# Due dates and measured ways in a hand-written planner: the first two blocks of a convolution with ELU layers

## The chip, the cores and the metric

One core of one Trainium2 chip runs the whole kernel as one launch. The metric is device time in microseconds (us) of that launch: the median of several runs. Engines are named PE (TensorE), DVE (VectorE), ACT (ScalarE), POOL (GpSimd) and SP (SyncE, which here only issues transfers).

## The reference

The inputs are x of 4 x 4096 x 192 and generated weights of 4 x 4096 x 8 x 7. Each token takes the softmax of its seven weights per head, and sums the last seven tokens with them (a causal convolution whose weights differ by token). The result goes through two matrices with an ELU between them:

```python
w = np.exp(weight_gen - np.max(weight_gen, axis=-1, keepdims=True))
w = w / (np.sum(w, axis=-1, keepdims=True) + 1e-09)
x_pad = np.concatenate([np.zeros((B, K - 1, D)), x], axis=1)
x_unf = x_pad[:, np.arange(S)[:, None] + np.arange(K)[None, :], :].reshape(B, S, K, H, D // H)
y = np.einsum('bshk,bskhg->bshg', w, x_unf).reshape(B * S, D)
h = y @ w_in                      # 192 x 2048
g = np.where(h > 0.0, h, np.exp(np.minimum(h, 0.0)) - 1.0)
out = g @ w_out                   # 2048 x 192
```

## The kernel before

The 16384 tokens go through in 32 blocks of 512, and each block takes 8 steps, one for each pair of 128-wide slices of the 2048 hidden units: 256 steps. A step multiplies into two PSUM banks of a ring of four (`h`, line 661, or line 657 for the two halves of step 0), ACT and DVE make the ELU of them (lines 718 to 732), and two steps later PE multiplies the result with w_out (line 689) into accumulator banks.

Block 0 multiplies in plain fp32, with decoded weights (`m_in`, `m_out`). From block 1 on every operand is split into two fp32r parts, hi and lo.

The matrices arrive as 64-bit floats and are turned into fp32 on the core. A piece of w_in or w_out is loaded by SP (lines 349, 384), ACT reads its two words (309, 312), DVE does three operations on it (315, 318, 321), and POOL adds the last part (331 for w_in, 325 for w_out). This happens beside block 0, piece by piece.

The convolution of blocks 0 and 1 is summed on PE: DVE makes a product `v` (line 555) for each of the seven taps and each half of the tokens, and PE adds it up with the identity matrix (line 542), in one bank for each half (`acc`, `accd`). Of block 0's second half POOL does the last three taps (`pa`, `pb`, lines 484 and 526). From block 2 on the convolution is on POOL. The products of block 0 read the softmax weights from a PSUM bank, which line 467 fills; ACT copies them to `wg` (line 470) for POOL. The result is transposed by DVE (line 605) and, for block 0, copied across partition halves by ACT and DVE (line 622).

Before any data is there, PE runs 21 multiplications of the identity matrix with itself (`turn_over`, line 402).

What sets the order is `Plan`. Every instruction, or small group, is a task with an engine and an estimated cost. A task that has a due date hands it back to the tasks it needs, less its cost and the way from engine to engine (`HOP`, or `SAME` within one engine). The tasks are then placed in the order of their due dates, each in the first free gap of its engine, and emitted in the order of the starts that this gives. Every engine runs its own instructions in that order. `port` is a resource that POOL tasks and some DVE tasks hold one at a time. The planned times have no other effect: waits on the chip follow the data.

Step k is due at 15,500 ns plus `FIRST[k]` for the first eleven steps and then one `STEP` (4,396 ns) after the other. `FIRST` thus places the early work against each other, and all later work against the early work.

Of the kernel before, what the change touches and what calls it, by code (L numbers as in the profile page):

```python
# [22 lines left out]
class Ring:  # L23


    def __init__(self, pool, shape, dtype, name, bufs):
        self.make = lambda dtype=dtype: pool.tile(
            list(shape), dtype, tag=name, name=name, bufs=bufs)
        self.bufs, self.made = bufs, []
# [23 lines left out]
class Plan:  # L53
# [4 lines left out]

    HOP = {"hop": 200, "dma": 2200, "pe": 250, "act": 220, "dve": 220, "pool": 220}
    SAME = {"hop": 0, "dma": 0, "pe": 0, "act": 60, "dve": 60, "pool": 60}

    def __init__(self):
        self.tasks = []

    def add(self, engine, cost, run, reads=(), writes=(), due=None, port=False):
        t = Task(engine, cost, run, due, port or engine == "pool")
        for h in reads:
            t.needs.update(h.writers)  # L70
        for h in writes:
            t.needs.update(h.users)
            if not h.users:
                if h.make:
                    t.makes.append(h)
                if h.before:
                    t.needs.update(h.before.users)
        for h in (*reads, *writes):
            h.users.append(t)
        for h in writes:  # L80
            h.writers.append(t)
        t.needs.discard(t)
        t.at = len(self.tasks)
        self.tasks.append(t)
        return t

    def lag(self, a, b):

        return self.SAME[a.engine] if a.engine == b.engine else self.HOP[a.engine]

    def issue(self):
        for t in self.tasks:
            for n in t.needs:
                n.next.append(t)
        for t in reversed(self.tasks):
            due = [n.due - t.cost - self.lag(t, n) for n in t.next]
            if t.due is not None:
                due.append(t.due)
            t.due = min(due)
        taken = {e: [(-1, 0)] for e in (*self.HOP, "port")}  # L100

        def fit(busy, at, cost):

            i = bisect.bisect_right(busy, (at, float("inf"))) - 1
            at = max(at, busy[i][1])
            while i + 1 < len(busy) and busy[i + 1][0] < at + cost:
                i += 1
                at = max(at, busy[i][1])
            return at

        for t in sorted(self.tasks, key=lambda t: (t.due, t.at)):
            uses = [taken[e] for e in ((t.engine, "port") if t.port else (t.engine,))]
            at = max([n.start + n.cost + self.lag(n, t) for n in t.needs], default=0)
            while True:
                to = at
                for busy in uses:
                    to = fit(busy, to, t.cost)
                if to == at:
                    break
                at = to  # L120
            t.start = at
            for busy in uses:
                bisect.insort(busy, (at, at + t.cost))
        self.emit(sorted(self.tasks, key=lambda t: (t.start, t.due, t.at)))
# [9 lines left out]
def conv_elu_kernel(  # L134
# [11 lines left out]
    nc = tc.nc  # L146
# [29 lines left out]
    PLAIN = 8  # L176
    EARLY = {0: 2500, 1: 1000}
    SPARE = 4
    FIRST = (0, 2667, 5719, 10622, 15932, 27986, 36877, 42127, 47378, 52168, 57525)
    ON_VEC = range(5, NF // 2)  # L180

    def rows(ap, t0, n):

# [49 lines left out]
    r_acc = [ring(f"acc{i}", [P, N], 1, pool=ps) for i in range(2)]  # L233
    r_accd = [ring(f"accd{i}", [P, N], 1, pool=ps) for i in range(2)]

    plan = Plan()
    add = plan.add

    idle = r_acc[0].new()
# [168 lines left out]
    def chunk(blk):  # L408

        n, t0 = J, blk * J * S  # L410
        xw, wg, wm, ws = r_xw.new(), r_wg.new(), r_wm.new(), r_ws.new()
        wg_h[blk] = wg
        xw_h[blk] = xw
        k, kk = n * H, n * H * K

        def w():
            return wg.t[:, 0:n]

        def wide(h):
            return h.t.to_broadcast([P, n, H, K])  # L420

        def load(to, src, n, d, at=0, both=False, only=quadrants()):
            def run():
                for p, s, q in only:
                    eng = nc.scalar if both and q else nc.sync
                    eng.dma_start(out=to()[p], in_=rows(src, t0 + s * J + at, n)[  # L426
                        :, :, q * d:(q + 1) * d])
            return run

        def load_w(only=quadrants()):  # L430
            return load(lambda: w().rearrange("p t h k -> p t (h k)"), weight_gen, n, H * K,
                        both=blk == 0, only=only)

        if blk == 0:
            add("dma", max(dma(P * n, H * K * 4), Q * S * ISSUE // 2), load_w(), writes=[wg], due=-2)
        for one in quadrants() if blk else ():
            add("dma", max(dma(A * n, H * K * 4), ISSUE), load_w([one]), writes=[wg])
        if blk == 0:
            xw_h[blk] = xw = [xw, Handle()]
            m = n + HALO  # L440
            for i, (a, b) in enumerate(((0, m - JH), (m - JH, m))):
                add("dma", max(dma(P * (b - a), DQ * 4), Q * S * ISSUE),
                    load(lambda a=a, b=b: xw[0].t[:, a:b], x, b - a, DQ, a),
                    writes=[xw[i]], due=-1 + i)
        else:
            for one in quadrants():
                add("dma", max(dma(A * (n + HALO), DQ * 4), ISSUE),
                    load(lambda: xw.t, x, n + HALO, DQ, only=[one]), writes=[xw])
        add("dve", dve(kk), lambda: nc.vector.tensor_reduce(
            out=wm.t[:, :, :, 0], in_=w(), axis=AX.X, op=ALU.max), reads=[wg], writes=[wm])  # L450
        add("dve", dve(kk), lambda: nc.vector.tensor_tensor(
            out=w(), in0=w(), in1=wide(wm), op=ALU.subtract), reads=[wm], writes=[wg], port=True)
        add("act", act(kk), lambda: nc.scalar.activation(
            out=w(), in_=w(), func=ACTF.Exp), writes=[wg])
        add("dve", dve(kk), lambda: nc.vector.tensor_reduce(
            out=ws.t[:, :, :, 0], in_=w(), axis=AX.X, op=ALU.add), reads=[wg], writes=[ws])
        add("act", act(k), lambda: nc.scalar.activation(
            out=ws.t, in_=ws.t, func=ACTF.Copy, bias=1e-9), writes=[ws])
        add("dve", 6.4 * k + 60, lambda: nc.vector.reciprocal(out=ws.t, in_=ws.t),
            writes=[ws])  # L460
        if blk == 0:
            h = wb_h[blk] = r_h.new()

            def bank():
                return h.t[:, 0:kk].rearrange("p (t h k) -> p t h k", h=H, k=K)

            add("dve", dve(kk), lambda: nc.vector.tensor_tensor(
                out=bank(), in0=w(), in1=wide(ws), op=ALU.mult), reads=[ws, wg], writes=[h],
                port=True)
            add("act", act(kk, True), lambda: nc.scalar.copy(out=w(), in_=bank()),  # L470
                reads=[h], writes=[wg])
            return
        add("dve", dve(kk), lambda: nc.vector.tensor_tensor(  # L473
            out=w(), in0=w(), in1=wide(ws), op=ALU.mult), reads=[ws], writes=[wg], port=True)
# [30 lines left out]
    def summed(blk, s0, own):  # L505
# [6 lines left out]
        xws = xws if blk == 0 else [xws]  # L512
        xw = xws[0]
        cs = [r_acc[1].new(), r_accd[1].new()]
        wb = [wb_h[blk]] * 2 if blk == 0 else cs[::-1]
        w0 = JH * DQ
        WK = JH * H * K
        rests = []
# [10 lines left out]
            rests.append(rest)  # L529

        def bank_w(i):
            at = i * WK if blk == 0 else w0
            return wb[i].t[:, at:at + WK]

        for i in range(2) if blk else ():
# [323 lines left out]
    with tc.manual_schedule():  # L859

        nc.vector.memset(scratch, 0.0)
        add("act", 1500, lambda: nc.scalar.activation(out=scratch, in_=scratch, func=ACTF.Exp),
            due=2500)
        make_identity(nc, ident)
        turn_over(21)
        for s in range(len(todo) + LAG):
            now = todo[s] if s < len(todo) else None
            up = todo[s - LAG] if s >= LAG else None
            if now:
                blk, k = now  # L870
                if k == 0:
                    chunk(blk)
                    if blk < 2:
                        summed(blk, s, OWN[blk])
                    else:
                        conv(blk, s)
                if blk == 0:
                    if k in in_pieces:
                        weights_in(k, in_pieces[k])
                    weights_out(k)  # L880
            period(s, now, up)
            if up and up[1] == NP - 1:
                drain(up[0], s)
        plan.issue()
# [34 lines left out]
```

## Time and profile before

| | us |
|---|---|
| median of 3 runs (1166.26 to 1166.52) | 1166.32 |
| the profiled execution, its own time | 1165.96 |
| its span, first to last instruction | 1164.2 |

The profile is of one execution; its own time is 1.76 us more than the span. PE is busy for 99% of the span, DVE for 71%, ACT for 77% and POOL for 59%. A matmul's end is modelled, so a wait of PE shows best in the distance from one group's start to the next. The profiler counts an fp32 matmul as two records. Matmuls of the two partition halves (64*128) run side by side.

### The profile page before, as it was taken

What the parts mean: (1) busy time and instruction counts of PE and PEld (TensorE: products, weight loads), DVE (VectorE), ACT (ScalarE), POOL (GpSimd) and SP (SyncE); (2) the same over time, 40 slices, a digit from 0 to 9 for tenths busy, and PEclk for the clock granted to TensorE, in tenths of its full rate; (3) what the DMA queues carried; (4) which work ended last, traced back from release to release, by engine and by line L of the source; (5) the groups of instructions that cost most, each with busy time, mean ns of one, the idle gap of its engine ahead of it and who ended that gap; (6) DMA issues with size and microseconds to landing.
All of it is one profiled execution on the core that took longest, in us unless ns stands there. A gap on an engine that the chain in (4) does not pass through costs nothing.

```text
span 1164.2 us, 32346 instructions
## 1 busy us (share of the span) xinstructions
PE 1157.0 (99%) x12858; PEld 1053.8 (91%) x12858; DVE 828.8 (71%) x1501; ACT 894.8 (77%) x1794; POOL 690.1 (59%) x424
## 2 busy tenths in 40 slices
PE   9999999999999999999999999999999999999998
PEld 6689999999999999999998999999999999999997
DVE  7967767866776776776787677687677776667564
ACT  6768778878777778777877777887877877777775
POOL 4576596388559858658859858756567655500000
PEclk9999999999999999999999999999999999999999
DMA  7831233323323332213332223332222211111100
GB/s 185 171 71 42 56 70 70 70 48 68 80 46 67 70 70 47 62 33 70 70 70 60 60 50 69 71 69 57 63 50 47 65 43 30 28 29 42 42 16 15
DMA packets 143128, 71.05 MB, mean 61 GB/s; under 512 B 98816, under 2 KB 141824, under 8 KB 142976
## 3 DMA queue, kind: packets, MB, share of 16 engines
q1 hardware_dynamic: 142112, 68.72, 26.7%
q8 instruction: 101, 1.65, 0.6%
q14 instruction: 51, 0.42, 0.1%
q10 hardware_dynamic: 864, 0.25, 0.1%
HBM read 31.98 MB, written 12.58 MB: 38 GB/s over the span
## 4 chain that ended last, share of the span: by engine, by line
PE 96%; DVE 2%; SPq 1%; DMA 0%; issue 0%; ACT 0%; POOL 0%; DVEq 0%; POOLq 0%; ACTq 0%
PE h L661 46%; PE accd L689 25%; PE acc L689 25%; PE accd L542 0%; SPq L426 0%; SPq L349 0%; DVE v L555 0%; DMA raw_in<-in_moe_w_in 0%; DVE hi L723 0%; DVE m_in L321 0%; DMA xw<-in_x 0%; DVE lo L730 0%; ACT e L718 0%; POOL m_in L331 0%; DVE m_in L318 0%
## 5 line engine op out<-in xcount | busy, mean ns | idle before, releaser
L723 DVE SCALAR_TENSOR_TENSOR h<-e,h 128x512 f32<-128x512 f32 x496 | 319.8, 690 | 221.1 <-ACT e L720 221.0
L718 ACT ACTIVATE e<-h 128x512 f32<-128x512 f32 x512 | 278.6, 595 | 184.6 <-PE h L661 184.4
L661 PE MATMUL h<-xhi,WI 64*128 64x512 f32 x2976 | 417.4, 394 | 0.1
L730 DVE TENSOR_TENSOR lo<-h,hi 128x512 fp32r<-128x512 f32 x496 | 322.1, 685 | 87.4 <-ACT hi L728 81.9
L661 PEld LDWEIGHTS h<-xhi,WI 64*128 64x128 f32 x2976 | 302.9, 185 | 47.8 <-DVE lo L730 0.7
L689 PE MATMUL accd<-WO,hi 64*128 64x384 f32 x1984 | 330.9, 357 | 0.0
L689 PE MATMUL acc<-WO,hi 64*128 64x384 f32 x1984 | 329.6, 355 | 0.0
L728 ACT CAST hi<-h 128x512 fp32r<-128x512 f32 x496 | 278.1, 597 | 41.7 <-DVE h L723 34.1
L720 ACT ACTIVATE e<-e 128x512 f32<-128x512 f32 x512 | 299.0, 644 | 0.1
L689 PE MATMUL acc<-WO,lo 64*128 64x192 f32 x1984 | 293.6, 249 | 0.0
L689 PE MATMUL accd<-WO,lo 64*128 64x192 f32 x1984 | 292.8, 248 | 0.0
L500 POOL TENSOR_TENSOR pa<-pa,pb 128x768 f32<-128x768 f32 x150 | 282.0, 1880 | 13.5 <-DVE pb L484 2.0
L484 POOL TENSOR_TENSOR pb<-xw,wg 128x768 f32<-128x768 f32 (+1 forms) x179 | 277.1, 1548 | 12.1
L689 PEld LDWEIGHTS acc<-WO,hi 64*128 64x128 f32 x1984 | 242.3, 185 | 4.5
L689 PEld LDWEIGHTS acc<-WO,lo 64*128 64x128 f32 x1984 | 237.6, 187 | 2.4
L661 PE MATMUL h<-xlo,WI 64*128 64x512 f32 x1488 | 239.3, 390 | 0.0
L689 PEld LDWEIGHTS accd<-WO,lo 64*128 64x128 f32 x1984 | 237.6, 188 | 0.0
L689 PEld LDWEIGHTS accd<-WO,hi 64*128 64x128 f32 x1984 | 233.5, 184 | 0.0
L661 PEld LDWEIGHTS h<-xlo,WI 64*128 64x128 f32 x1488 | 164.4, 184 | 28.2
L484 POOL TENSOR_TENSOR pa<-xw,wg 128x768 f32<-128x768 f32 (+1 forms) x31 | 47.5, 1532 | 176.2 <-DVE wg L473 148.1
L500 POOL TENSOR_TENSOR xc<-pa,pb 128x768 f32<-128x768 f32 x30 | 55.5, 1851 | 106.0 <-DVE xt L605 104.4
L605 DVE STREAM_TRANSPOSE xt<-xc 128x256 f32<-128x256 f32 x90 | 33.0, 416 | 1.4
(84 smaller groups left out, 495.2 us busy)
## 6 DMA issues: line engine op xcount, KB each, us to landing
xw<-in_x SPq DMA_DIRECT2D x124, 168.0 KB, 3.5
xhi<-xhi SPq DMA_DIRECT2D x62, 192.0 KB, 3.1
xlo<-xlo SPq DMA_DIRECT2D x62, 192.0 KB, 2.9
out_dram<-raw_out SPq DMA_DIRECT2D x124, 96.0 KB, 1.9
wg<-in_weight_gen SPq DMA_DIRECT2D x126, 28.0 KB, 2.2
raw_out<-in_moe_w_out SPq DMA_DIRECT2D x8, 384.0 KB, 5.9
raw_in<-in_moe_w_in SPq DMA_DIRECT2D x12, 192.0 KB, 4.3
raw_in<-in_moe_w_in SPq DMA_DIRECT2D x8, 96.0 KB, 2.5
```

Of the source, the lines that this page charges most:

```text
L484: lambda: eng.tensor_tensor(out=h.t[:, 0:J], in0=xw.t[:, j0 + k:j0 + k + J, :].rearrange("p j (h g) -> p j h g", g=G), in1=wg.t[:, j0:j0 + ...
L500: add("pool", pool(J * DQ), lambda b=b, to=to: nc.gpsimd.tensor_tensor(out=to.t, in0=a.t, in1=b.t, op=ALU.add), reads=[b] if to is a else ...
L605: nc.vector.transpose(out=xt(i)[:, c], in_=src[:, :, c * A:(c + 1) * A])
L661: return lambda: nc.tensor.matmul(out=h.t, lhsT=w_in_f[k][1]()[p, c] if w is None else WI[p, k, w, c], rhs=x.t[p, c, c0:c0 + 2].rearrange( ...
L689: return nc.tensor.matmul(out=to(), lhsT=src.t[p, g * P:(g + 1) * P], rhs=w, start=start, stop=False, skip_group_check=True).ins
L718: add("act", act(N, True), lambda: nc.scalar.activation(out=e.t, in_=h.t, func=ACTF.Relu, scale=-1.0), reads=[h], writes=[e])
L720: add("act", act(N), lambda: nc.scalar.activation(out=e.t, in_=e.t, func=ACTF.Exp, scale=-1.0), writes=[e])
L723: add("dve", dve(N), lambda: nc.vector.scalar_tensor_tensor(out=to.t, in0=e.t, scalar=-1.0, in1=h.t, op0=ALU.add, op1=ALU.max), reads=[e, ...
L728: add("act", act(N, True), lambda: nc.scalar.copy(out=hi.t, in_=h.t), reads=[h], writes=[hi])
L730: add("dve", dve(N), lambda: nc.vector.tensor_tensor(out=lo.t, in0=h.t, in1=hi.t.bitcast(F32), op=ALU.subtract), reads=[h, hi], writes=[lo])
```

## The change

It alters the numbers that the planner works with, and one piece of the program.

- `HOP` and `SAME`, the ways from engine to engine, have new values, and one from DVE to POOL its own.
- The costs of the first three loads, of the softmax weights and of the two parts of block 0's x, are other numbers.
- `FIRST` has new values; from the seventh entry on they are later, the last by 7,475 ns.
- `NUDGE` moves the due dates of 168 tasks forward, by 200 to 4,000 ns each. Tasks are named by their number in the order in which the program adds them; the numbers go from 12 to 682, which is into block 3. The task's forerunners inherit the earlier date.
- The softmax weights of block 0 are written into two PSUM banks, one for each half of the tokens, by two DVE instructions of 112 columns where there was one of 224. ACT copies the second half alone, since POOL reads nothing else.
- `turn_over` runs 14 multiplications instead of 21.

```diff
-    HOP = {"hop": 200, "dma": 2200, "pe": 250, "act": 220, "dve": 220, "pool": 220}
-    SAME = {"hop": 0, "dma": 0, "pe": 0, "act": 60, "dve": 60, "pool": 60}
+    HOP = {"hop": 200, "dma": 2200, "pe": 220, "act": 140, "dve": 130, "pool": 100}
+    SAME = {"hop": 0, "dma": 0, "pe": 0, "act": 20, "dve": 125, "pool": 65}
...
+        if a.engine == "dve" and b.engine == "pool":
+            return 220
...
-            t.due = min(due)
+            t.due = min(due) - self.nudge.get(t.at, 0)
...
-    FIRST = (0, 2667, 5719, 10622, 15932, 27986, 36877, 42127, 47378, 52168, 57525)
+    FIRST = (0, 2700, 5400, 10600, 15900, 28000, 37500, 42900, 48300, 55000, 65000)
...
+    NUDGE = {
+        12: 3400, 22: 2700, 32: 1800, 41: 2200, 44: 3700, 46: 2700, 48: 2000, 50: 2600, 56: 1400,
+        58: 3800, 67: 2500, 71: 1600, 72: 3800, 79: 1700, 84: 1400, 96: 2600, 97: 3000, 98: 1200,
...
+        470: 1600, 471: 2200, 472: 2500, 474: 2400, 475: 600, 476: 3200, 479: 3200, 480: 3500,
+        481: 1800, 482: 2700, 485: 1600, 486: 1100, 487: 1800, 488: 2700, 490: 200, 498: 2300,
...
-            add("dma", max(dma(P * n, H * K * 4), Q * S * ISSUE // 2), load_w(), writes=[wg], due=-2)
+            add("dma", 700 + Q * S * ISSUE // 2, load_w(), writes=[wg], due=-2)
...
-                add("dma", max(dma(P * (b - a), DQ * 4), Q * S * ISSUE),
+                add("dma", dma(P * (b - a), DQ * 4),
...
-            h = wb_h[blk] = r_h.new()
-
-            def bank():
-                return h.t[:, 0:kk].rearrange("p (t h k) -> p t h k", h=H, k=K)
-
-            add("dve", dve(kk), lambda: nc.vector.tensor_tensor(
-                out=bank(), in0=w(), in1=wide(ws), op=ALU.mult), reads=[ws, wg], writes=[h],
-                port=True)
-            add("act", act(kk, True), lambda: nc.scalar.copy(out=w(), in_=bank()),
-                reads=[h], writes=[wg])
+            wb_h[blk] = [r_h.new(), r_h.new()]
+            for i, h in enumerate(wb_h[blk]):
+                def half(t, i=i):
+                    return t[:, i * JH:(i + 1) * JH]
+
+                def bank(h=h):
+                    return h.t[:, 0:kk // 2].rearrange("p (t h k) -> p t h k", h=H, k=K)
+
+                add("dve", dve(kk // 2), lambda half=half, bank=bank: nc.vector.tensor_tensor(
+                    out=bank(), in0=half(w()), in1=half(wide(ws)), op=ALU.mult),
+                    reads=[ws, wg], writes=[h], port=True, due=due1(0) - 14000 + 1000 * i)
+                if OWN[blk][i] < K:
+                    add("act", act(kk // 2, True), lambda half=half, bank=bank: nc.scalar.copy(
+                        out=half(w()), in_=bank()), reads=[h], writes=[wg])
...
-        wb = [wb_h[blk]] * 2 if blk == 0 else cs[::-1]
+        wb = wb_h[blk] if blk == 0 else cs[::-1]
...
-            at = i * WK if blk == 0 else w0
+            at = 0 if blk == 0 else w0
...
-        turn_over(21)
+        turn_over(14)
```

## Rows read from the trace of the kernel before

**Rows 1.** The page: the span.

```profile
span 1164.2 us, 32346 instructions
```

**Rows 2.** Stretches: us, then busy us (count) of each engine, clock, DMA.

```profile
8.05:16.25 8.20, 7.96 (x27) 4.29 (x25) 8.08 (x19) 3.74 (x7) 5.58 (x6) 1.00 0.86 212
16.25:24.93 8.68, 8.59 (x49) 5.02 (x49) 8.26 (x15) 7.60 (x15) 4.26 (x5) 1.00 0.91 235
24.93:37.05 12.12, 12.11 (x105) 8.77 (x104) 11.64 (x24) 11.27 (x25) 6.56 (x7) 1.00 0.90 179
37.05:45.39 8.34, 7.57 (x25) 4.01 (x23) 8.27 (x19) 7.77 (x17) 5.38 (x7) 1.00 0.72 149
75.00:1100.00 1025.00, 1024.89 (x11672) 946.85 (x11670) 731.73 (x1318) 801.82 (x1609) 649.72 (x384) 1.00 0.26 58
```

**Rows 3.** Timeline of PE to 60 us: start, length, operation, count, wait.

```profile
8.05 4.73 PE L542 MATMUL acc<-v,ident 128*128 128x384 f32 x14
...
16.25 2.86 PE L657 MATMUL h<-xhi,m_in 64*128 64x256 f32 x24 [0.24 <-POOL m_in L331]
19.19 5.76 PE L661 MATMUL h<-xhi,m_in 64*128 64x512 f32 x24
...
26.33 2.74 PE L661 MATMUL h<-xhi,m_in 64*128 64x512 f32 x12
...
31.68 2.85 PE L661 MATMUL h<-xhi,m_in 64*128 64x512 f32 x12
...
37.05 4.78 PE L542 MATMUL acc<-v,ident 128*128 128x384 f32 x14
42.61 2.85 PE L542 MATMUL accd<-v,ident 128*128 128x384 f32 x8 [0.77 <-DVE v L555]
45.39 2.85 PE L661 MATMUL h<-xhi,m_in 64*128 64x512 f32 x12
...
53.00 2.74 PE L661 MATMUL h<-xhi,m_in 64*128 64x512 f32 x12
...
55.58 0.32 PE L689 MATMUL acc<-m_out,hi 64*128 64x192 f32 x1
...
58.18 2.74 PE L661 MATMUL h<-xhi,m_in 64*128 64x512 f32 x12
```

**Rows 4.** Timeline of the first 10 us, all engines.

```profile
1.36 6.86 PE L402 MATMUL acc<-ident 128*128 128x128 f32 x42 [1.36 <-POOL ident masks.py:199]
...
6.58 0.40 DVE L467 TENSOR_TENSOR h<-wg,ws 128x224 f32<-128x224 f32 x1
7.01 0.56 DVE L555 TENSOR_TENSOR v<-xw,h 128x384 f32<-128x384 f32 x1
7.66 0.34 ACT L470 COPY wg<-h 128x224 f32<-128x224 f32 x1 [1.50 <-DVE v L555]
...
8.04 2.41 DVE L555 TENSOR_TENSOR v<-xw,h 128x384 f32<-128x384 f32 x5 [0.47 <-ACT wg L470]
```

**Rows 5.** Stretches, line 402 alone: us, PE and PEld busy (count), clock.

```profile
1.36:5.36 4.00, 4.00 (x19) 4.00 (x19) 1.00 0.81 154
5.36:8.05 2.69, 2.69 (x25) 2.66 (x24) 1.00 0.70 165
```

**Rows 6.** Timeline of DVE, 12 to 43 us.

```profile
18.30 1.26 DVE L318 TENSOR_SCALAR m_in<-m_in 128x768 int32<-128x768 int32 x1
...
20.77 1.28 DVE L723 SCALAR_TENSOR_TENSOR hi<-e,h 128x512 f32<-128x512 f32 x2 [0.21 <-ACT e L720]
...
28.76 0.54 DVE L318 TENSOR_SCALAR m_in<-m_in 128x768 int32<-128x768 int32 x1
...
41.13 0.96 DVE L321 SCALAR_TENSOR_TENSOR m_in<-raw_in,m_in 128x768 int32<-128x768 int32 x1
```

**Rows 7.** Timeline of two steps of a middle block.

```profile
311.18 1.28 DVE L730 TENSOR_TENSOR lo<-h,hi 128x512 fp32r<-128x512 f32 x2
...
313.37 1.56 PE L661 MATMUL h<-xhi,WI 64*128 64x512 f32 x12
```

More of the change, by code (lines that the diff above doesn't have):

```diff
@@ L53, with __init__ @@
 class Plan:
-    HOP = {"hop": 200, "dma": 2200, "pe": 250, "act": 220, "dve": 220, "pool": 220}
-    SAME = {"hop": 0, "dma": 0, "pe": 0, "act": 60, "dve": 60, "pool": 60}
-    def __init__(self):
-        self.tasks = []
+    HOP = {"hop": 200, "dma": 2200, "pe": 220, "act": 140, "dve": 130, "pool": 100}
+    SAME = {"hop": 0, "dma": 0, "pe": 0, "act": 20, "dve": 125, "pool": 65}
+    def __init__(self, nudge):
+        self.tasks, self.nudge = [], nudge
     def add(self, engine, cost, run, reads=(), writes=(), due=None, port=False):
@@ L234, in conv_elu_kernel @@
     r_accd = [ring(f"accd{i}", [P, N], 1, pool=ps) for i in range(2)]
-    plan = Plan()
+    plan = Plan(NUDGE)
     add = plan.add
```

17 rows, old and new, of the table NUDGE are left out of this document.

## The prediction

> **What bounds the kernel now.** I read the stretches first. From 75 to 1100 us PE is busy for 1024.89 of 1025.00 us [rows 2]: from there on PE alone sets the pace, and an order that is already good enough there can only be kept or spoiled. So a gain has to come from the first 75 us, and the next question is how much PE loses in them. The busy column doesn't tell, since ends are modelled; the distances between starts do [rows 3]. The clean paces are: 12 records of line 661 take 2.58 us (53.00 to 55.58), 32 records of line 689 take 2.60 (55.58 to 58.18), and a record of line 542 takes 0.326 us (its row of 14 is 4.73 long; less the 0.16 by which the row of 2.74 outlasts its 2.58). The 24 half-width records of step 0 have the columns of 12 whole ones, so I count them at 2.58. Then:
>
> - 8.05 to 26.33 is 18.28 us. The work in it is 24 records of line 542 (7.82), step 0 (2.58), steps 1 and 2 (5.16), 16 records of line 689 (1.30): 16.86. Lost: 1.42.
> - 26.33 to 45.39 is 19.06. Two lots of 12 plus 32 records (10.36) and 22 of line 542 (7.17) make 17.53. Lost: 1.53, and 0.77 of it is one wait, for a product `v` of DVE.
> - 45.39 to 53.00 is 7.61, for 5.18 and 6 records of line 542 (1.96). Lost: 0.47.
>
> That is 3.42 us of waiting in all, and it is nearly everything that an order can win, beside an earlier start than 8.05. The third view says who is late. DVE is busy for 8.08 of 8.20, 8.26 of 8.68, 11.64 of 12.12 and 8.27 of 8.34 us in the four stretches up to 45.39, POOL for little more than half [rows 2]. So PE waits for DVE, and DVE has almost no slack of its own there: a better order can make DVE do the urgent thing first, but it can't make it do more. The wait of 0.77 shows how: the decoding of a w_in piece (41.13, 0.96 us) stands ahead of the product that PE waits for [rows 3, 6].
>
> **The change part by part.**
>
> *Warm-up and banks.* PE runs its 42 identity records until 8.05, where the first conv record starts, although the product it needs is done at 7.01 + 0.56 = 7.57 [rows 3, 4]. So the warm-up itself holds PE. Its records come at two paces: 19 touch the first 4.00 us and 25 the next 2.69, about 0.21 and 0.11 us each [rows 5]. The clock column says 1.00 for both, so it is the halving of the distance that shows the lower level (1.2 GHz) and then the upper (2.4 GHz), at about 5.4 us. With 14 calls, 28 records, the last 9 or 10 run at the upper level and the warm-up ends near 6.5. DVE's multiply takes 0.40 us for 224 columns, and 0.56 for 384 [rows 4], so about 1.0 ns a column and some 0.29 for 112. The first product then ends 0.11 earlier, at 7.46, and PE starts near 7.50: **0.55 us earlier**.
>
> For DVE the two banks do more. Today ACT's copy (7.66 to 8.00) reads the bank that the products read, the copy starts after the first product and DVE stands still for 0.47 us until it is over [rows 4]. With a bank for each half, the first half is read by DVE alone: 0.47 saved, and 0.18 lost, as two multiplies of 0.29 replace one of 0.40. By the due dates in the diff the second half's multiply (nudged by 3,400) comes out at -12.7 us, between the second product (-15.3) and the third (-12.0). POOL's three products so start a little later than now; POOL works 5.58 of 8.20 us in that stretch [rows 2], so the 2.6 us that are free cover it. Without them PE would wait for the POOL sum at the end of the conv.
>
> *Ways, load costs, FIRST and NUDGE.* None of these is an instruction; each acts only by changing the order on an engine. The new ways fit the trace: from the multiply to the product it is 0.43 us, where the plan now has 303 + 125 and had 303 + 60; from the copy's start to the next product it is 0.38, where the plan now has 257 + 140 and had 257 + 220 [rows 4]. So the plan will be nearer to what happens, and what it moves should mostly hold. SP's first transfers keep their order, since weights and x still come due long before w_in. What the moved dates are worth can't be read from the diff, so I bound each stretch.
>
> Up to 26.33: DVE is the limit, so the start 0.55 us earlier doesn't all arrive. Sure is 0.47 - 0.18 = 0.29. To be had are also a wait of 0.21 for ACT, and one operation of line 318 that took 1.26 us where the same shape took 0.54 [rows 6]; together 1.22. Above that lies only the cap, 1.42 + 0.55 = 1.97. I take 0.9, nearer to the 1.22, as the plan sees each of these.
>
> 26.33 to 45.39: between nothing and 1.53. I take the wait of 0.77, which is plainly one of order, and half of the other 0.76: 1.15.
>
> 45.39 to 53.00: between nothing and 0.47; half, 0.24.
>
> *The sum* is 0.9 + 1.15 + 0.24 = 2.3 us. The profiled execution took 1165.96 us, 1.76 more than its span [rows 1], and so would come to 1163.7; it lies 0.36 below the median of 1166.32, and on the median the sum gives **1164.0**. If DVE gave only the sure 0.29, it would be 1166.0, and with nothing left to wait for (3.42 + 0.55) 1162.35.
>
> **The rivals.**
>
> *The gain is given back (0.2 to 1.2 us, 1165.1 to 1166.1).* DVE is busy all the way to 45 us, so an urgent thing moved forward pushes another back, and PE waits for that instead. For it: the four stretches above. Against it: the 0.77 us wait stands behind decoding that is needed only two POOL operations later. One form of this rival is the clock. The shorter warm-up leaves PE with nothing between about 6.5 and 7.5 us. If the clock fell there and took as long to rise as at the start, 4.00 us at half pace, PE would lose 2.0 of the 2.3 us: 1166.0. Against it, PE stood for 0.77 us before 42.61 and its 8 records after that have 2.78 us to the next group, at the upper pace [rows 3]. The Trainium skill ("TensorE: Matmul & The Clock Gate", "HAM oscillation — how this bites in real kernels") warns that waits between bursts of matmuls put the array back to half rate, and by it a hole cut into the warm-up is a risk. The trace has no hole that did so.
>
> *Slower: the later blocks' order is spoiled.* The ways act on all 256 steps, and no nudge reaches beyond block 3. In a middle block the last subtraction of line 730 frees its bank at 311.18 + 1.28 = 312.46 and PE takes it at 313.37 [rows 7]: 0.91 us to spare. The new ways make the plan's chain from PE over ACT, ACT, DVE, ACT to DVE shorter by 0.32 us (30, 40, 80, 90 and 80 ns by the diff), so other DVE work may be put in front of that subtraction. From 0.91 us of it PE waits. If a block had that once, by 0.2 us, 29 blocks would cost 5.8 us: 1166.3 - 2.3 + 5.8 = 1169.8. For it: DVE is 71% busy over this stretch, 731.73 of 1025.00 [rows 2], so the work isn't spread thin. Against it: 0.32 is a third of what there is to spare, and PE shows no wait there now.
>
> *Nearly all of the waiting goes (over 3.7 us, under 1162.6).* The search had the same plan to work on that now fits the trace. Against it: DVE's full stretches.
>
> **How the numbers follow.** What a measurement of this kernel tells from no change is about 0.2%, 2.3 us; my sum lies on that line. The forecast, a gain of 1.2 to 3.7 us (1162.6 to 1165.1), has 0.59, and I split it 0.37 to 0.22 at 2.3 us, because the gains that are surest (the bank, the start, the 0.77 wait) come first and the search adds to them. Gain given back: 0.20, 0.04 of it by the clock. Nearly all gone: 0.07. Slower: 0.14, of which 0.02 too little to tell. So faster is 0.37 + 0.07 = 0.44, same 0.22 + 0.20 + 0.02 = 0.44, slower 0.12. The likeliest case alone spans 1162.6 to 1165.1. For 8 in 10 the range goes from 1162.2, the cap, where little is left out below, to 1167.0, which takes in the given-back gain and the smallest of the losses.
>
> **What will show it.** In the changed kernel's profile: the first record of line 542 at 7.5 instead of 8.05 and at the upper pace; no idle time of DVE between the first products; the start of step 3 (26.33) near 25.4; no wait of PE for a product near 42; the step at 53.00 near 50.7; and from there the same distances as now up to a span near 1161.9. The prediction is wrong if PE's starts in the first 53 us are earlier by less than 1 us or more than 3.7, if PE's records up to 12 us come at half pace, or if waits of PE turn up after 75 us.

## The result: slower by 0.66%, and the profile after

The changed kernel takes 1173.47 us (median of 6 runs, 1173.12 to 1176.28) where the kernel before takes 1166.29 beside it: ratio 1.0066, 95% interval 1.0053 to 1.0079. That is 7.2 us lost where 2.3 us of gain were forecast. The profiled execution took 1173.36 us. The page of after, its span and its shares by slices:

```profile
span 1171.6 us, 32289 instructions
...
PEclk9998999999999999999999999999999999999999
```

The span is 7.4 us longer than in [rows 1]. The fourth digit of the clock row, the slice that holds 100 us, shows less than full speed in a stretch where before had no loss. The stretches of after (columns as in [rows 2]):

```profile
75.00:104.00 29.00, 25.70 (x256) 23.07 (x255) 26.41 (x36) 19.82 (x39) 27.65 (x18) 0.88 0.31 70
75.00:1100.00 1025.00, 1020.28 (x11574) 928.92 (x11573) 747.00 (x1303) 811.05 (x1592) 645.19 (x384) 1.00 0.25 56
```

The second row answers the last of [rows 2]: PE is busy for 1020.28 us instead of 1024.89. The first row says where most of that is. In before the same 29 us read:

```profile
75.00:104.00 29.00, 29.00 (x334) 26.77 (x332) 21.38 (x39) 21.86 (x45) 17.25 (x12) 1.00 0.31 70
```

PE idles for 3.3 us and its clock falls to 0.88 on average, while DVE is 5 us busier with three instructions fewer and POOL is busy for 27.65 us instead of 17.25. The view of waits of PE in after (engine, tile, line waited for: us in total, times, longest):

```profile
PE h L689 <- DVE lo L758: 3.3, 1, 3.3
...
PE accd L717 <- SPq L704: 1.2, 1, 1.2
```

The timeline of PE in after answers [rows 3]:

```profile
1.36 5.86 PE L426 MATMUL acc<-ident 128*128 128x128 f32 x28 [1.36 <-POOL ident masks.py:199]
7.44 4.78 PE L570 MATMUL acc<-v,ident 128*128 128x384 f32 x14 [0.23 <-DVE v L583]
...
17.69 1.57 PE L685 MATMUL h<-xhi,m_in 64*128 64x256 f32 x12 [0.71 <-DVE xhi L650]
...
19.62 2.85 PE L689 MATMUL h<-xhi,m_in 64*128 64x512 f32 x12 [0.36 <-POOL m_in L355]
...
23.70 2.74 PE L689 MATMUL h<-xhi,m_in 64*128 64x512 f32 x12
...
44.23 4.78 PE L570 MATMUL accd<-v,ident 128*128 128x384 f32 x14
...
54.22 2.74 PE L689 MATMUL h<-xhi,m_in 64*128 64x512 f32 x12
...
61.98 1.24 PE L689 MATMUL h<-xhi,WI 64*128 64x512 f32 x8
...
96.45 3.58 PE L689 MATMUL h<-xhi,WI 64*128 64x512 f32 x12 [3.30 <-DVE lo L758]
```

Steps from 8 on (the first whose w_in product reads `WI`) come in one order in both kernels. But the w_out records do not stand between the same steps everywhere, and this alone moves the start of a single step by up to 1.8 us; so I subtract only the starts of steps that have the same records ahead of them in both. In before, step 15 starts here:

```profile
93.87 1.57 PE L661 MATMUL h<-xhi,WI 64*128 64x512 f32 x12
```

Step 8 starts at 61.98 instead of 63.22 (1.24 earlier) and step 10 1.43 earlier. So the front did win, up to about six tenths of the forecast. Then step 15 is 2.58 late (96.45 for 93.87), step 19 5.49, step 25 7.04, and the last step 7.63. Nearly the whole loss sits between steps 14 and 25, and the largest part of it in one hole of PE.

**What DVE does before that hole.** The timeline of DVE in after, from 83 us:

```profile
83.60 0.73 DVE L501 TENSOR_TENSOR wg<-wg,ws 128x224 f32<-128x224 f32 x1
84.25 0.68 DVE L751 SCALAR_TENSOR_TENSOR h<-e,h 128x512 f32<-128x512 f32 x1
84.85 1.52 DVE L307 TENSOR_TENSOR WI<-m_in,WI 128x384 fp32r<-128x384 f32 x1
...
86.66 1.53 DVE L307 TENSOR_TENSOR WI<-m_in,WI 128x384 fp32r<-128x384 f32 x1
88.11 0.68 DVE L751 SCALAR_TENSOR_TENSOR h<-e,h 128x512 f32<-128x512 f32 x1
...
90.11 1.82 DVE L307 TENSOR_TENSOR WI<-m_in,WI 128x384 fp32r<-128x384 f32 x1
91.86 2.59 DVE L643 TENSOR_TENSOR xlo<-xt,xhi 128x768 fp32r<-128x768 f32 x1
94.37 1.28 DVE L751 SCALAR_TENSOR_TENSOR h<-e,h 128x512 f32<-128x512 f32 x2
95.70 1.35 DVE L758 TENSOR_TENSOR lo<-h,hi 128x512 fp32r<-128x512 f32 x2
```

The `lo` that PE waits for stands behind two `h`, and these behind a subtraction of 1.82 and one of 2.59 us. In the groups by line and shape (count, then busy us and mean ns), before needs 551 ns for a `WI` subtraction and 957 for `xlo`:

```profile
L283 DVE TENSOR_TENSOR WI<-m_in,WI 128x384 fp32r<-128x384 f32 x3 | 1.5, 551 | 0.0
L615 DVE TENSOR_TENSOR xlo<-xt,xhi 128x768 fp32r<-128x768 f32 x1 | 1.0, 957 | 0.0
```

Beside the slow ones POOL, in after:

```profile
84.41 1.55 POOL L512 TENSOR_TENSOR pa<-xw,wg 128x768 f32<-128x768 f32 x1 [0.33 <-DVE wg L501]
85.91 1.86 POOL L512 TENSOR_TENSOR pb<-xw,wg 128x768 f32<-128x768 f32 x1
87.85 2.04 POOL L528 TENSOR_TENSOR pa<-pa,pb 128x768 f32<-128x768 f32 x1
89.98 1.54 POOL L512 TENSOR_TENSOR pb<-xw,wg 128x768 f32<-128x768 f32 x1
91.60 2.03 POOL L528 TENSOR_TENSOR pa<-pa,pb 128x768 f32<-128x768 f32 x1
93.71 2.14 POOL L512 TENSOR_TENSOR pb<-xw,wg 128x768 f32<-128x768 f32 x1
```

and in before:

```profile
95.50 1.55 POOL L484 TENSOR_TENSOR pa<-xw,wg 128x768 f32<-128x768 f32 x1 [11.28 <-DVE wg L473]
```

Here is the fault. Block 3's convolution on POOL starts once DVE has multiplied the block's softmax weights. In before DVE does that at 95.03, after block 2's subtractions, and POOL stands still for 11.28 us until then. In after it does it at 83.60, ahead of them, and POOL runs without a pause while DVE subtracts. The two columns of starts show what that costs: at 85.91, 87.85, 91.60 and 93.71 POOL goes from one instruction to the next, and the three slow `WI` and the `xlo` end at 86.37, 88.19, 91.93 and 94.45, that is 0.34 to 0.46 and 0.74 us later. So each seems to do its work only once POOL's instruction has ended, and the POOL instruction after it is the longer one (1.86 and 2.14 for a product of 1.54, 2.04 for a sum of 1.84). `h` and `lo`, with one operand in PSUM, keep to 688 and 689 ns (688 and 686 in before). The Trainium skill ("SBUF — State Buffer", "Who interferes with whom") says that a VectorE instruction with two SBUF inputs contends with a GpSimd instruction that reads SBUF, because its second input comes through a read interface that the two share, and that the shared ports are an exclusive lock; the trace agrees, with these four ends.

**What the hole costs.** Stretches of after:

```profile
92.00:96.40 4.40, 1.15 (x14) 0.91 (x10) 4.35 (x5) 1.25 (x3) 4.24 (x3) 0.88 0.12 29
96.40:98.00 1.60, 1.55 (x5) 1.08 (x7) 1.60 (x2) 1.54 (x3) 1.52 (x2) 0.50 0.90 233
98.00:100.00 2.00, 2.00 (x12) 1.51 (x12) 2.00 (x3) 0.63 (x1) 1.92 (x2) 0.50 0.22 54
100.00:102.00 2.00, 2.00 (x16) 1.80 (x14) 1.88 (x3) 1.21 (x3) 1.92 (x2) 0.50 0.00 0
102.00:104.00 2.00, 2.00 (x30) 2.00 (x29) 1.36 (x3) 1.97 (x4) 1.92 (x2) 0.97 0.00 0
```

The clock falls inside the hole and stays at the lower level (1.2 GHz) until 102.1, so PE runs 5.7 us of work at half pace: 2.8 us more. With the starts less the work in them, as in the prediction's first part, after loses 6.5 us from 90 to 110 (3.3 of the hole and 2.8 of the clock are in it) and 1.6 from 120 to 140 (with the 1.2 us wait for SP's hop). That is 8.1 us, and from step 10 to step 25 PE falls back by 8.47. That hop is the same fault again: at 129.47 block 3's `xlo` takes 2.46 us beside POOL's convolution of block 4, SP's transfer of line 661 waits 1.9 us for it, and the hop (an instruction of SP that does nothing but pass a dependency on) stands behind that transfer in SP's queue, so PE waits.

### The profile page after: what moved, and what is told of

The parts are those of the page before. It is cut to its first block, busy times and chain, and to the rows that moved or that the text cites. A ratio compares the mean times of both kernels' runs of the same rounds, so it can differ in the third digit from the quotient of the medians.

```text
span 1171.6 us, 32289 instructions
## 1 busy us (share of the span) xinstructions
PE 1159.6 (99%) x12844; PEld 1041.7 (89%) x12844; DVE 858.0 (73%) x1502; ACT 913.7 (78%) x1794; POOL 687.5 (59%) x424
## 4 chain that ended last, share of the span: by engine, by line
PE 94%; DVE 2%; ACT 1%; SPq 1%; DMA 1%; issue 0%; DVEq 0%; ACTq 0%
PE h L689 45%; PE accd L717 24%; PE acc L717 24%; ACT hi L756 0%; SPq L450 0%; DVE xlo L643 0%; DMA raw_out<-in_moe_w_out 0%; ACT e L748 0%; PE accd L570 0%; PE acc L570 0%; SPq L373 0%; DMA raw_in<-in_moe_w_in 0%; DVE WI L307 0%; DVE h L751 0%; ACT e L746 0%
## 5 line engine op out<-in xcount | busy, mean ns | idle before, releaser
L689 PEld LDWEIGHTS h<-xhi,WI 64*128 64x128 f32 x2976 | 274.1, 186 | 58.0 <-DVE lo L758 4.2
L717 PE MATMUL acc<-WO,hi 64*128 64x384 f32 x1984 | 305.8, 355 | 0.2 <-SPq L704 0.2
L717 PE MATMUL acc<-WO,lo 64*128 64x192 f32 x1984 | 254.1, 249 | 0.0
L717 PE MATMUL accd<-WO,lo 64*128 64x192 f32 x1984 | 253.8, 248 | 0.0
L689 PE MATMUL h<-xlo,WI 64*128 64x512 f32 x1488 | 214.8, 391 | 0.0
L717 PEld LDWEIGHTS acc<-WO,lo 64*128 64x128 f32 x1984 | 193.8, 187 | 5.2
L717 PEld LDWEIGHTS acc<-WO,hi 64*128 64x128 f32 x1984 | 191.7, 185 | 6.2 <-SPq L704 0.9
L717 PEld LDWEIGHTS accd<-WO,lo 64*128 64x128 f32 x1984 | 194.8, 188 | 0.1
L717 PEld LDWEIGHTS accd<-WO,hi 64*128 64x128 f32 x1984 | 191.9, 184 | 1.8 <-SPq L704 1.4
L643 DVE TENSOR_TENSOR xlo<-xt,xhi 128x768 fp32r<-128x768 f32 (+1 forms) x32 | 33.8, 1058 | 1.2
```

The costliest lines, as they stand in the source:

```text
L643: add("dve", dve(C * n * A), lambda i=i: nc.vector.tensor_tensor(out=to(xlo, i), in0=xt(i), in1=to(xhi, i).bitcast(F32), op=ALU.subtract), ...
L689: return lambda: nc.tensor.matmul(out=h.t, lhsT=w_in_f[k][1]()[p, c] if w is None else WI[p, k, w, c], rhs=x.t[p, c, c0:c0 + 2].rearrange( ...
L717: return nc.tensor.matmul(out=to(), lhsT=src.t[p, g * P:(g + 1) * P], rhs=w, start=start, stop=False, skip_group_check=True).ins
```

## The experiments

Theory A: the loss is POOL's early convolution beside DVE's subtractions (and the clock with it). Theory B: it is the moved order of the first blocks as a whole. Theory C: the new ways spoil the later blocks' order, as in the prediction's slower rival. Ratios are to runs of the kernel before on the same chip.

**thin3.** The changed kernel, in which all but the first product and the last sum of block 3's convolution on POOL touch one of 8 token columns; the rest of block 3's convolution is left out.

```
-            lambda: eng.tensor_tensor(
-                out=h.t[:, 0:J],
...
+            lambda n=1 if blk == 3 and k else J: eng.tensor_tensor(
+                out=h.t[:, 0:n],
```

> The changed kernel in its own order, but GpSimd's convolution of block 3 works on one of eight token columns in all but its first product and its last sum, so block 3's output is wrong; everything else is unchanged. Theory A (port): VectorE's SBUF subtractions near 85 to 100 us take 1.5 us instead of 0.55 because GpSimd works beside them; with GpSimd nearly idle they take about 0.55, PE's wait of 3.3 us and the fall of the clock go, and the time is 1164 to 1167. Theory B (order): the nudged order itself puts too much VectorE work ahead of what PE needs; the wait stays and the time stays within 2 us of 1173.5.

Measured: 1168.51 us, ratio 1.0017 (1.0007 to 1.0026). Its span is 1165.6, PE's wait for `lo` and the fall of the clock are gone (29 us at 1.00), and step 19 starts 1.01 earlier than before instead of 5.49 later. DVE's groups in 75 to 104 us of thin3:

```profile
L307 DVE TENSOR_TENSOR WI<-m_in,WI 128x384 fp32r<-128x384 f32 x3 | 2.6, 859 | 0.0
L645 DVE TENSOR_TENSOR xlo<-xt,xhi 128x768 fp32r<-128x768 f32 x1 | 1.1, 1108 | 0.0
```

Same DVE order, same early start of POOL (83.98), little POOL work: the subtractions are short but for the one beside the full first product (1.52). It takes back 5.0 of the 7.2 us, and ends 1.5 us above theory A's range: the hop's wait of 1.2 us is still there, and step 25 stands 0.55 late.

**hold3.** The changed kernel, in which block 3's multiply also waits for block 2's split and for the subtractions on DVE.

```
+        late = [*(w_in_h[k][1] for k in ON_VEC), *(w_out_h[pair_of[k][0]][1] for k in ON_VEC),
+                *xt_h[2]] if blk == 3 else []
-            ..., op=ALU.mult), reads=[ws], writes=[wg], port=True)
+            ..., op=ALU.mult), reads=[ws, *late], writes=[wg], port=True)
```

> The changed kernel, with block 3's last softmax multiply made to wait in the plan for block 2's split and for the six subtractions of w_in and w_out that VectorE does, so that GpSimd starts block 3's convolution after them. Nothing is left out. Theory A (port): 1164 to 1167, the first-75-us gain of about 1.3 us kept, perhaps less 1 us if the same meeting recurs between blocks 3 and 4. Theory B (order): VectorE's order up to 92 us is the same but for one instruction of 0.4 us, so PE still waits and the time stays above 1171. Theory C (new ways spoil all later blocks): above 1171 too.

Measured: 1168.18 us, ratio 1.0012 (1.0003 to 1.0021). All the work is done and one thing is put back, and 5.3 of 7.2 us return, to 1.2 us above theory A's range. POOL starts block 3 at 101.07; DVE's groups in 75 to 104 us of hold3:

```profile
L307 DVE TENSOR_TENSOR WI<-m_in,WI 128x384 fp32r<-128x384 f32 x3 | 1.6, 535 | 0.0
L645 DVE TENSOR_TENSOR xlo<-xt,xhi 128x768 fp32r<-128x768 f32 x1 | 0.9, 950 | 0.0
```

Step 19 is 0.90 earlier than before and step 26 still 0.88 earlier, but by the end it is 2.26 late. The waits of PE in hold3 name about half of that drift:

```profile
PE acc L719 <- SPq L706: 1.7, 4, 0.6
```

These are four waits of 0.2 to 0.6 us for SP's hop, before 432, 679, 715 and 926 us: small losses far behind the last moved date.

**early3.** The kernel before, in which one task has a due date: block 3's last softmax multiply.

```
-            ..., op=ALU.mult), reads=[ws], writes=[wg], port=True)
+            ..., op=ALU.mult), reads=[ws], writes=[wg], port=True,
+            due=80000 if blk == 3 else None)
```

> The kernel before with one due date more: block 3's last softmax multiply is due at 80 us, so that VectorE does it ahead of the subtractions of w_in and w_out instead of behind them, and GpSimd starts block 3's convolution near 85 instead of 95 us. Nothing is left out, ways, banks and warm-up are as before. Theory A (GpSimd beside VectorE's SBUF subtractions): these take about 1.5 us each and block 2's low part about 2.5, some 8 us more of VectorE's time, PE waits in 85 to 105 us; 2 to 8 us slower, 1168 to 1174. Theory B (the nudged order as a whole): no change beyond 0.5 us, since all else is in the order of before.

Measured: 1172.69 us, ratio 1.0054 (1.004 to 1.0068): 6.4 of the 7.2 us, from one date in the kernel before. The waits of PE, then the stretch, then DVE's groups in it:

```profile
PE h L662 <- DVE lo L731: 2.5, 2, 2.3
```

```profile
75.00:104.00 29.00, 25.83 (x262) 22.13 (x259) 25.30 (x32) 17.90 (x36) 28.06 (x18) 0.94 0.31 70
```

```profile
L283 DVE TENSOR_TENSOR WI<-m_in,WI 128x384 fp32r<-128x384 f32 x3 | 5.5, 1876 | 0.0
L283 DVE TENSOR_TENSOR WO<-m_out,WO 128x384 fp32r<-128x384 f32 x3 | 4.5, 1561 | 0.0
L616 DVE TENSOR_TENSOR xlo<-xt,xhi 128x768 fp32r<-128x768 f32 x1 | 2.3, 2272 | 0.0
```

Much as in after: subtractions 2.4 to 3.4 times as long, POOL busy for 28 of 29 us, PE short by 3.2. Step 8 stands within 0.1 us of before, step 19 is 6.61 late and the last 6.71. The planner also orders DVE's work in later blocks otherwise for this date, but from step 19 on only 0.1 us is lost. B and C can't make this loss, as neither the other moved dates nor the new ways are in this kernel. Theory A holds.

**no_nudge and old_ways** ask what brought the multiply forward. The first is the changed kernel without its moved dates (`Plan({})`); the second has them, but the ways of the kernel before (`HOP`, `SAME`, no case for DVE to POOL).

> The changed kernel with no due date moved: new ways, load costs, FIRST, two banks and 14 warm-up calls stay. In this order block 3's GpSimd convolution stands behind VectorE's subtractions again. Theory A: no overlap, no long subtraction, 1165 to 1167, as the start is earlier and the rest is near the order of before. Theory C (ways): 1170 or more, as these ways act on all blocks.

> The changed kernel with the ways from engine to engine of before; nudges, FIRST, load costs, two banks and 14 calls stay. In this order block 3's multiply stands behind VectorE's subtractions. Theory A: no meeting on the port, part of the front gain kept: 1165.0 to 1167. If the nudges themselves make the loss (theory B): 1172 or more.

Measured: no_nudge 1167.06, ratio 1.0006 (0.9997 to 1.0015); old_ways 1168.13, ratio 1.0016 (1.0007 to 1.0025). POOL's first product of block 3 in no_nudge, then in old_ways:

```profile
99.74 1.54 POOL L512 TENSOR_TENSOR pa<-xw,wg 128x768 f32<-128x768 f32 x1 [14.30 <-DVE wg L501]
```

```profile
99.29 1.54 POOL L510 TENSOR_TENSOR pa<-xw,wg 128x768 f32<-128x768 f32 x1 [13.35 <-DVE wg L499]
```

Neither alone brings it forward; the two together do. Each has a small loss of its own: no_nudge is 0.79 late at step 8 and 1.16 at the end, old_ways 0.24 late at step 8 and 3.0 at the end, of which 2.6 come from 133 to 150 us, in waits of PE and its weight loads of up to 0.5 us each, most of them for DVE's `lo`. (Its longest wait, 1.5 us for ACT's `xhi`, is at 17.8 us.) no_nudge lies at the upper edge of theory A's range, old_ways 1.1 us above it. So the moved dates are worth about 2 us at step 8 (0.79 late without them, 1.24 early with them). The new ways without the dates cost nothing that can be told from no change, so as the cause of the 7.2 us theory C falls. A small loss of its kind remains: from step 30 to the end the kernels whose later blocks are planned with the new ways fall back by 0.5 to 2.9 us (no_nudge 0.5, after 0.6, thin3 1.1, hold3 2.9, and hold34, below, 2.2), and those planned with the old ways (early3, old_ways and all others below) by at most 0.35. That is one execution of each, and no run tests it by itself.

**banks and b14** try the parts at the start. banks is the kernel before with the two banks and the 14 calls; b14 is the kernel before with the 14 calls alone (`turn_over(14)` for `turn_over(21)`).

> The kernel before with the two banks, the single copy and 14 warm-up calls alone; ways, costs, FIRST as before, no nudges. The first convolution matmul comes at 7.5 instead of 8.05 us at the upper clock, VectorE has no idle time between its first products. By the prediction's first term 0.3 to 0.9 us faster: 1165.4 to 1166.0. If the shorter warm-up cost the clock, records near 8 to 12 us would come at half pace and the time would be 1167 or more.

> The kernel before with 14 calls of the warm-up instead of 21, nothing else. If the shorter warm-up alone brings the earlier start, the first convolution starts near 7.6 instead of 8.05 us; DVE sets the pace behind it, so little of the 0.4 us arrives: 1165.9 to 1166.4. If it leaves a hole before the convolution in which the clock falls, or the clock has not risen by then, 1166.8 to 1168.

Measured: banks 1167.27 (1166.92 to 1169.03), ratio 1.0013 (1.0004 to 1.0023); b14 1165.70, ratio 0.9996 (0.9986 to 1.0005). The timeline of PE in b14, and one of its waits:

```profile
1.35 5.26 PE L402 MATMUL acc<-ident 128*128 128x128 f32 x28 [1.35 <-POOL ident masks.py:199]
7.33 1.94 PE L542 MATMUL acc<-v,ident 128*128 128x384 f32 x4 [0.72 <-DVE v L555]
```

```profile
PE accd L542 <- DVE v L555: 0.8, 1, 0.8
```

PE starts 0.72 earlier, still waits 0.8 near 42 us, as in [rows 3], and 0.25 is left at the last step: DVE sets the pace behind the start, as the prediction had it. That 0.25 lies within what can be told from no change. In banks PE starts at 7.31, and steps 3 and 4 are 0.58 and 0.76 earlier, but then its conv 1 waits for DVE:

```profile
PE accd L568 <- DVE v L581: 2.0, 1, 2.0
```

in place of the 0.77 of [rows 3], and step 8 is 0.87 late: the gain is given back, and the forecast of 0.3 to 0.9 us faster was wrong. In that stretch two decodings of DVE that stand ahead of the product take 1.24 and 1.15 us, where the same shapes take 0.56 and 0.35 elsewhere in the run; both lie beside subtractions of POOL and end 0.42 and 0.22 after one of these ends, so this is a collision of the same kind as in theory A. The 10 runs of banks spread over 2.1 us, and the four longest have the lower granted clocks (0.997 to 0.999 on the mean); whether the wait of 2.0 us made the clock fall in these four isn't shown.

**splice, hold34, two_plans, two_plans21 and two_plans30** try to keep the new front and the old rest. hold34 is hold3 with the same condition on block 4. The others plan twice, with and without the moved dates and new ways (both times with the `FIRST` of before), and join the two lists: splice at task 450, the two_plans kernels at task 635, near the beginning of block 3, with block 3's multiply held behind DVE's subtractions in the first two; two_plans21 has 21 calls. two_plans30 joins the old list 3.0 us earlier instead of 2.0, without the hold.

```
+        self.place(self.WAYS[0], self.nudge)
+        for t in self.tasks:
+            t.key = t.start, t.due
+        self.place(self.WAYS[1], {})
+        for t in self.tasks:
+            if t.at >= self.CUT:
+                t.key = t.start - self.BACK, t.due
...
+        self.emit(sorted(self.tasks, key=lambda t: (*t.key, t.at)))
```

> Two plans in one: the tasks up to step 15 in the order of the changed plan, block 2's preparation and all later work in an order planned with the ways of before and without nudges, 1.5 us earlier. Two banks and 14 calls stay. If the front gain of 1.2 to 1.9 us at step 8 to 10 is lasting and the later losses come from the later order alone: 1164.5 to 1165.5, faster than both. If something else is lost with the shorter front: 1166 or more.

> As the hold of block 3, and block 4's multiply also waits in the plan for block 3's split. If the wait of PE for a hop on SyncE near 130 us in the changed kernel comes from block 3's low part, which takes 2.46 instead of 0.96 us beside GpSimd's block 4, the wait is gone there as it is with block 3 held; the waits of 0.4 to 0.6 us on hops in later blocks stay, and the time is that of the first hold within 0.7 us: 1167.5 to 1168.9.

> The change with its new order kept only up to the first sums of block 3; from there on every engine has the order of the kernel before, and block 3's multiply is put behind the subtractions of block 2. If the loss comes only from POOL's convolution of block 3 beside DVE's subtractions and from the new ways in the later blocks, and the new front is worth its 1.2 to 1.4 us, the gain of step 10 stays to the end: 1165.0 to 1165.8 us, the hops' waits gone. If the waits in the later blocks come whenever the front is shifted, whatever the order behind it: 1166.5 to 1168.

> As two_plans, with the 21 calls of the warm-up as in the kernel before. If the shorter warm-up is what brings the earlier start, the first convolution starts near 8.0 instead of 7.4 us and the time is 0 to 0.6 us longer than that of two_plans. If the shorter warm-up costs a later rise of the clock, the records up to 10 us come at the upper pace here and the two times are equal or this one is shorter.

> As two_plans, but the order of the kernel before is joined on 3.0 us earlier instead of 2.0 and block 3's multiply has no added condition, so that DVE's sequence around it (the last subtractions of w_out, reciprocal, multiply) is that of the kernel before. If two_plans lost its 9 us because the multiply, and with it POOL's convolution of block 3, came 6.5 us late (102.07 instead of 95.50), POOL starts block 3 near 94.5 here, the waits for SP's hops after 120 us go, and the 0.6 to 1.4 us of the front stay to the end: 1165.0 to 1166.0 us. If a shifted front makes such waits whatever stands behind it, they are here too: 1167 or more.

Measured: splice 1167.36, ratio 1.001 (1.0001 to 1.0018); hold34 1168.04, 1.0016 (1.0007 to 1.0025); two_plans 1175.11, 1.0073 (1.006 to 1.0085); two_plans21 1175.91, 1.0081 (1.0067 to 1.0094); two_plans30 1172.56, 1.0049 (1.0035 to 1.0062). None beats before. hold34 takes away the hop's wait near 130 us and is 1.04 ahead at step 26, but drifts to 1.44 late as hold3 does. splice is 1.14 ahead at step 8, has lost that by step 15 and is 1.42 late from step 20 on. The two_plans kernels fail at their seam. In the first, POOL starts block 3 at 102.07, 6.6 us later than before, and the waits of SP (112 to 126 us) and of PE read:

```profile
SPq L468 <- POOL pb L534: 5.5, 1, 5.5
```

```profile
PE acc L739 <- SPq L726: 4.3, 1, 4.3
```

SP's loads for a later block wait for a buffer that the late convolution still reads, the hop that PE needs stands behind them, and PE stops for 4.3 us, after which its clock is at 0.78 on average from 125 to 140 us. hold3 starts POOL's block 3 at 101.07 without such a stop, so the lateness alone doesn't make it; the order in SP's queue may do its part, which no run tests. two_plans21 starts its convolution at 7.89 instead of 7.30 and is 0.8 us slower than two_plans, which the few runs of each don't tell apart. In two_plans30 POOL comes at 100.44, against an expected 94.5, and PE has by then waited 2.8 us for another hop, until 83.20 (step 15 is 5.22 late), with the clock at 0.83 from 80 to 100 us. The forecasts of two_plans and two_plans30 were wrong, and whether the new front can be kept to the end stays open: no run here kept it.

## Why the prediction was wrong

*The start was right.* The first convolution record starts at 7.44 (7.50 forecast) at the upper pace, and DVE's idle time of 0.47 [rows 4] is gone. The form of the given-back rival in which the hole behind the shorter warm-up drops the clock didn't come. In after there was hardly a hole for it: the 28 warm-up records lasted until 7.22 (6.5 forecast), 0.23 before the convolution. In b14 the hole was 0.72, and the time didn't rise.

*Up to step 8: right in kind, one term too large.* 2.3 us were summed and 1.24 came at step 8 (1.43 at step 10). Counted as in the prediction, starts less the work ahead of them, the second and third term came nearly as forecast. From 23.70 to 44.23 after loses 0.4 us in place of 1.53, so 1.1 was won where 1.15 was forecast, with the wait of 0.77 for `v` gone; from 44.23 to 54.22 it loses 0.25 in place of 0.47, so 0.2 for 0.24. The first term (0.9) came to next to nothing. The 0.6 us of the earlier start came, but up to 23.70, the step behind the first 16 records of w_out, PE loses 1.98 us (16.26 less 14.28 for 24 records of the convolution, steps 0 and 1 and those 16), where before loses 1.42 up to 26.33; that leaves 0.05: two new waits, 0.71 for DVE's `xhi` and 0.36 for POOL's `m_in`, took the place of the old ones, as the given-back rival says of a DVE that is full.

*The step that failed* is the one on the time after 75 us. The prediction's sum puts that time at nothing, and where the text says that an order which is good enough there "can only be kept or spoiled", it puts the spoiling to the ways alone, all over the middle blocks, at line 730's 0.91 us [rows 7]. It notes that no nudge reaches beyond block 3, and doesn't ask what they move up to there. The spoiling was in one place, where POOL's convolution of block 3, and then of block 4, meets DVE's subtractions; the dates and the ways together brought it there, and it cost some 8 us by step 25. Its price was in no term: a DVE subtraction beside POOL's convolution costs 1.5 to 1.9 us instead of 0.55, and 2.6 instead of 0.96, and PE's hole of 3.3 us took 2.8 more by the clock. The range's upper end, 1167.0, leaves no room for it. From step 25 on, over 230 steps, after lost only 0.6 us.

*The trace of before had said it twice.* [Rows 6] show one operation of DVE (a TENSOR_SCALAR, with a single tensor operand) at 1.26 us and the same shape at 0.54; the prediction booked the difference as a gain "to be had" and didn't ask what made it. POOL's timeline of before has this row beside it:

```profile
17.93 1.21 POOL L331 TENSOR_TENSOR m_in<-m_in,raw_in 128x384 int32<-128x384 int32 x1 [1.74 <-DVE m_in L321]
```

It ends at 19.14, and DVE's 1.26 us, from 18.30, end 0.42 later; at 28.76, where the same takes 0.54, POOL stands still. POOL's idle 11.28 us at 84 to 95 us, just while DVE subtracts, ended by DVE's multiply, was a gap that an earlier date for that multiply would fill. The statement that the ways fit the trace better, so that what the plan moves "should mostly hold", missed that the plan's own costs for DVE and POOL don't overlap: it lets one of them use the port at a time and leaves POOL a gap of 1.8 us for a `WI` and the `xlo` (its list has POOL's first two products of block 3 at 84.20 and 87.54). In the trace POOL waits for nothing there and starts its second product at 85.91; the gap doesn't exist, and the subtractions run beside POOL.

*What would show it wrong* did: waits of PE after 75 us.

## What to carry to other kernels

When an order moves, look at every engine that it wakes earlier, and ask what runs beside it: here a POOL that stood idle for 11 us was what kept DVE fast. Price an operation at both durations that the trace shows (alone, and beside the other engine), and treat a spread of 0.54 to 1.26 us for one shape as a question. A planner that keeps two engines off one resource only by its planned times keeps them off only while the chip keeps to those times; hold3's dependency kept POOL's convolution away from these subtractions whatever the times.

## What had not been expected of the hardware

- DVE instructions with two SBUF operands wait for POOL's running instruction to end: 551 to 1626 (after) and 1876 ns (early3) for 128x384, 957 to 2587 and 2272 for 128x768, mean of a group. The length of POOL's instruction counts: with most of them short (thin3, 0.35 to 1.0 us) the means are 859 and 1108, and without the one beside the full first product the two left of 128x384 take 0.51 and 0.55 us.
- The decoding's TENSOR_SCALAR on SBUF, with one tensor operand, does it too: 1.26 for 0.54 us in before, 1.24 for 0.56 and 1.15 for 0.35 in banks.
- A hole of 3.3 us in PE cost 2.8 us more by the clock in after. In two_plans (4.3) and two_plans30 (2.8) the clock also fell within the hole; in early3 (2.3) it fell 1.5 us after the hole had ended (1.00 from 96.6 to 98, 0.53 from 98 to 100 us); in banks, with a hole of 2.0 us, the clock of the profiled execution is 1.00. The Trainium skill ("TensorE: Matmul & The Clock Gate", "HAM oscillation — how this bites in real kernels") tells of waits between bursts of matmuls that put the array back to half rate; after agrees, with 0.50 in the three stretches behind the hole.
- SP's queue carries a POOL or DVE delay to PE: transfers that waited 1.9 and 5.5 us held back hops, and PE stood for 1.2 and 4.3 us.
